# Two buffers for two output tiles and products for two taps in the last stage of a fused forward and backward kernel

## The chip, the cores and the metric

The kernel runs on one core of a Trainium2 chip. The metric is device time in microseconds (us), from runs on the chip, with the median of several. A profiled execution gives one trace, with times counted from the start of its span. The engines are TensorE (PE, with its weight loads as PEld), VectorE (DVE), ScalarE (ACT), GpSimd (POOL) and SyncE (SP), which mostly issues DMAs. Each engine runs its instructions in the order in which they were put into its queue.

## The reference

The forward pass adds a residual, a long convolution gated by a layer norm (an H3 block, A) and a bilinear gated feed-forward block (B). The kernel returns its output and the gradients of nine inputs for a given `grad_out`. The shapes are S = 2048 rows, D = 512 columns, F = 1376 hidden columns, 4 shift taps, all in bf16.

```python
xn = layernorm(A_q)
# A: q = xn
k_shift[s] = sum over t of k[s - 3 + t] * shift_k[:, 3 - t]
kv = k_shift * v
y = irfft(rfft(kv, 2S) * rfft(ssm_k, 2S))[:S] + kv * ssm_D
# B
h = (xn @ w_gate) * (xn @ w_up)
out = A_q + xn * y + h @ w_down
# returned: out, and its gradients by A_q, A_k, A_v, A_shift_k, A_ssm_k, A_ssm_D, w_gate, w_up, w_down
```

For the part that is changed, these lines matter. With `dks` the gradient by `k_shift`, the gradient by k is a sum of four products, row s being `sum over j of dks[s + j] * shift_k[:, j]`. The gradient by `shift_k` is, for each tap, the sum over the rows of `dks` times the shifted k. The gradient by A_q is a layer-norm backward pass over `grad_out * y` plus the feed-forward's part, plus `grad_out` itself.

## The kernel before

Rows are laid out as 128 partitions with R = 16 rows each, so a pass b from 0 to 7 works on the two rows 2b and 2b + 1 of every partition, and an operation on both rows has 128x1024 elements.

The work has three stages. The first (to about 110 us) normalises, makes the tables of the discrete Fourier transform and does the first halves of the transforms. The second (to about 300 us) runs the feed-forward block chunk by chunk (`ffn1`, `yb`) with the spectral products in between (`g_fwd`, `g_mul`, `g_inv`); its products land in DRAM (`HDD`, `BX`, `GD`). The third stage, which holds all of the change, starts with the line `wy_es.close()` and runs from about 316 us. There the main generator `dw()` takes the eleven hidden blocks fb in turn: `down_grad(fb)` (tile pd, gradient of w_down), transposes of the hidden values (`hid_t`, tile pt; for the last three blocks a transposing DMA, tile natT, and `last_t`), and the gradients of w_gate and w_up (tile pu). At each `yield` of `dw()` four side generators are moved on by a table of start and step:

```python
sides = [every(seq(inv_y(), load_dk()), 0, 3), every(dsk_gram(), 27, 2), every(inv_dk(), 35, 3), every(ew(), 10, 3)]
```

- `inv_y()` finishes the inverse transforms: `st1p` makes the tiles yC and dd through PSUM tile pq, and VectorE multiplies dd with v into `dks` (L948) and with the shifted k into kb (L949), which is stored to out_3. The last two calls use rows 12 to 15.
- `dsk_gram()` makes the gradient by `shift_k`: for each of four column groups TensorE fills the PSUM tile pk from `dks` and k (khC), VectorE takes its diagonal into the tile kd (L1077) and sums it (L1079); at the end dskb is transposed (pts) and copied into dskt.
- `inv_dk()` makes the gradient by ssm_k (tiles po, o5t) and, in `put_dD`, the gradient by ssm_D (ptd, dDt).
- `ew()` runs the list `tail`: final(0), final(1), bwd(0), final(2), bwd(1), and so on to final(7), bwd(6), bwd(7). `final(b)` makes two rows of the output (tile o) and of the gradient by A_q (tile e, with a float32 tile dxn), from yC, xnC, goC and a tile bb that `load_fin` loads from BX one pass ahead. `bwd(b)` makes two rows of the gradient by k (tile dk, with the tile tk for a product).

The stores of o, e and dk are not issued by the pass itself: they go into the list `late` and are issued by `put_late()` at the beginning of the next pass, on SP's queue. Nearly every other DMA of this stage is on that queue too. The DMAs use eight completion semaphores in rotation, so a DMA waits for the landing of the one that used its semaphore before.

The order of instructions on each engine isn't the order of the program text: the tile framework schedules them by priority, with its own estimate of times, and blocks under `tc.high_priority(offset=SOON)` are drawn forward. Buffers come from pools: c2 has one buffer for each name (`bufs=1`), c2b two; a new tile under a name (or a `tag`) waits until all readers of the tile that had the buffer before are done, a store's DMA among them. The last half of the last `down_grad` is copied by VectorE and stored by SP:

```python
for h, cp, q in ((0, act, nc.scalar), (1, dve, nc.sync)):
    hc = slice(256 * h, 256 * h + 256)
    cp(od[:fw, hc], pd[:fw, hc])
    q.dma_start(out_9[f0:f0 + fw, hc], od[:fw, hc])
```

Of the kernel before, what the change touches and what calls it, by code (L numbers as in the profile page):

```python
# [8 lines left out]
BF = mybir.dt.bfloat16  # L9
F32 = mybir.dt.float32  # L10
I32 = mybir.dt.int32
ALU = mybir.AluOpType
# [6 lines left out]
D = 512  # L19
F = 1376  # L20
R = 16
P = 128
NC4 = 4
# [167 lines left out]
def kernel(  # L191
# [24 lines left out]
    nc = tc.nc  # L216
# [20 lines left out]
    def dve(o, i):  # L237
        nc.vector.tensor_copy(o, i)  # L238
# [13 lines left out]
    def P2(name, shape, dt=F32):  # L252
        return ps2.tile(shape, dt, name=name, tag="p2")

    def P1(name, shape, dt=F32):
        return ps1.tile(shape, dt, name=name, tag="p1")
# [5 lines left out]
    skb = const.tile([P, 4, D], BF, name="skb")  # L262
# [640 lines left out]
    c2b = ctx.enter_context(tc.tile_pool(name="c2b", bufs=2, side="right", reuse_waits="tile"))  # L903
    c2 = ctx.enter_context(tc.tile_pool(name="c2", bufs=1, side="right", reuse_waits="tile"))
    yC = c2.tile([P, R, D], BF, name="yC")
    dks = c2.tile([P, R + 3, D], BF, name="dks")
# [158 lines left out]
    def dsk_gram():  # L1065
        for c in range(NC4):
            pk = P2("pk", [P, 2, D])
            for r in range(R):
                for h in range(2):
                    c0 = c * 128 + 64 * h  # L1070
                    nc.tensor.matmul(pk[64 * h:64 * h + 64, h, 0:256], lhsT=dks[:, r, c0:c0 + 64],
                                     rhs=KH[0][:, r:r + 4, c0:c0 + 64], start=(r == 0), stop=(r == R - 1))
            kd = c2.tile([P, 4, 64], F32, name="kd")
            with tc.high_priority(offset=SOON):
                for h in range(2):
                    hs = slice(64 * h, 64 * h + 64)
                    nc.vector.tensor_tensor(kd[hs], pk[hs, h, 0:256].rearrange("q (j c) -> q j c", j=4),  # L1077
                                            ident[hs, hs].unsqueeze(1).to_broadcast((64, 4, 64)), op=ALU.mult)
                nc.vector.tensor_reduce(dsk[:, c, :], kd[:], axis=AX.X, op=ALU.add)  # L1079
            yield  # L1080
        dskb = c2.tile([P, 4, NC4], BF, name="dskb")
        nc.vector.tensor_copy(dskb[:], dsk[:].rearrange("q c i -> q i c"))
        for _ in range(2):
            yield
        pt = P1("pts", [P, 4, P], BF)
        for j in range(4):
            nc.tensor.transpose(pt[:NC4, j, :], dskb[:, 3 - j, :], ident[:])
        dskt = c2.tile([NC4, P, 4], BF, name="dskt")
        dve(dskt[:], pt[:NC4].rearrange("c j q -> c q j"))
        nc.sync.dma_start(out_4.rearrange("(c p) j -> c p j", p=128), dskt[:])  # L1090
        yield

    def bwd(b):
        rb = slice(2 * b, 2 * b + 2)
        dk = c2b.tile([P, 2, D], BF, name="dk")
        t = c2.tile([P, 2, D], BF, name="tk", tag="dxn")
        for j in range(4):
            src = dks[:, 2 * b + j:2 * b + j + 2, :]
            w = skb[:, j:j + 1, :].to_broadcast((P, 2, D))
            if j == 0:  # L1100
                nc.vector.tensor_tensor(dk[:], src, w, op=ALU.mult)
            else:
                nc.vector.tensor_tensor(t[:], src, w, op=ALU.mult)  # L1103
                nc.vector.tensor_tensor(dk[:], dk[:], t[:], op=ALU.add)  # L1104
        late.append((o2_n[:, rb, :], dk))

    FL = {}
# [2 lines left out]
    def load_fin(b):  # L1110
        bb = c2b.tile([P, 2, 2, D], BF, name="bb")
        nc.sync.dma_start(bb[:], BX[:, 2 * b:2 * b + 2, :, :])
        FL[b] = bb

    def final(b):
        if b + 1 < 8:
            load_fin(b + 1)
        bb = FL.pop(b)
        rb = slice(2 * b, 2 * b + 2)
        tt = nc.vector.tensor_tensor  # L1120
        stt = nc.vector.scalar_tensor_tensor
        o = c2.tile([P, 2, D], BF, name="o0")
        tt(o[:], xnC[:, rb], yC[:, rb], op=ALU.mult)
        tt(o[:], o[:], bb[:, :, 0, :], op=ALU.add)
        late.append((o0_n[:, rb, :], o))
        e = c2.tile([P, 2, D], BF, name="e")
        tt(e[:], goC[:, rb], yC[:, rb], op=ALU.mult)
        dxn = c2.tile([P, 2, D], F32, name="dxn")
        for i in range(2):
            r = 2 * b + i  # L1130
            stt(dxn[:, i], e[:, i], 1.0, bb[:, i, 1, :], op0=ALU.mult, op1=ALU.add, accum_out=s1[:, r:r + 1])
            stt(e[:, i], dxn[:, i], 1.0, xnC[:, r, :], op0=ALU.mult, op1=ALU.mult, accum_out=s2[:, r:r + 1])
        nc.vector.tensor_scalar(m2[:, rb], s2[:, rb], -1.0 / D, None, op0=ALU.mult)
        stt(m1[:, rb], s1[:, rb], -1.0 / D, rstd[:, rb], op0=ALU.mult, op1=ALU.mult)
        for i in range(2):
            r = 2 * b + i
            stt(dxn[:, i], xnC[:, r, :], m2[:, r:r + 1], dxn[:, i], op0=ALU.mult, op1=ALU.add)
            nc.vector.tensor_scalar(e[:, i], dxn[:, i], rstd[:, r:r + 1], m1[:, r:r + 1], op0=ALU.mult, op1=ALU.add)
        tt(e[:], e[:], goC[:, rb], op=ALU.add)
        late.append((o1_n[:, rb, :], e))  # L1140
# [16 lines left out]
    for b in range(8):  # L1157
        tail.append(lambda b=b: final(b))
        if b > 0:
            tail.append(lambda b=b: bwd(b - 1))  # L1160
    tail.append(lambda: bwd(7))

    def put_late():
# [16 lines left out]
    def load_dk():  # L1180
        gks.append(load_gk(0))
        gks.append(load_gk(1))
        yield

    sides = [every(seq(inv_y(), load_dk()), 0, 3), every(dsk_gram(), 27, 2), every(inv_dk(), 35, 3), every(ew(), 10, 3)]
    for n, _ in enumerate(dw()):
        for sd in sides:
# [36 lines left out]
```

## Time and profile before

| what | us |
|---|---|
| median of 3 runs (lowest to highest) | 491.06 (489.58 to 493.37) |
| the profiled execution, its own time | 491.36 |
| its span | 489.6 |
| TensorE, weight loads busy | 470.8, 313.9 |
| VectorE, ScalarE, GpSimd busy | 341.1, 317.2, 15.4 |
| stage from 330 to 480: VectorE busy | 106.4 of 150 |
| bytes moved by DMA | 139.87 MB, 286 GB/s |

An engine's busy time is the sum of its instructions' time in the trace; matmuls are pipelined, so TensorE's is not a measure of its peak. The granted clock of TensorE is 0.99 on the mean. An engine's wait names what released it. A line such as L235 or L238 is that of the helper `act` or `dve`, through which all plain copies go, so copies are told apart by their tiles. "To landing" of a DMA counts from its issue to the moment at which its semaphore is set.

### The profile page before, as it was taken

Reading aid. Unit: us, or ns where it says so; the run is one execution under the profiler, and the core shown is the slowest. Engines: PE = TensorE matmul, PEld = TensorE weight load, DVE = VectorE, ACT = ScalarE, POOL = GpSimd, SP = SyncE. Lnnn points to the kernel's source line nnn. Section 1 sums busy time; section 2 is a strip of 40 time slices with the busy share of each in tenths; the row PEclk is TensorE's granted clock in tenths of the full one; section 3 lists DMA queues with packets and bytes.
Section 4 is the critical chain, followed back from the end, with each engine's and each line's share of the span. In section 5 each row is a group of like instructions: output and inputs, shape, how many; then the busy total and the mean of one; then the engine's idle time right before and its main releaser. Section 6 shows DMA issues by size and latency. Waiting matters only on the chain.

```text
span 489.6 us, 10516 instructions
## 1 busy us (share of the span) xinstructions
PE 470.8 (96%) x4335; PEld 313.9 (64%) x4335; DVE 341.1 (70%) x623; ACT 317.2 (65%) x353; POOL 15.4 (3%) x31
## 2 busy tenths in 40 slices
PE   7998999999999999999999999999999999999992
PEld 7866754547647457357357734577677778777790
DVE  6889979987275667677687873021270999998895
ACT  4876896769568678789689953567557522733320
POOL 8010000000000000000000000020000000000000
PEclk9999999999999999999999999999999999999996
DMA  8999999999997979788977199989999898999518
GB/s 272 376 380 347 304 257 330 330 317 327 313 300 229 255 233 242 242 260 251 287 240 239 62 368 321 352 313 350 325 367 362 301 326 270 311 310 229 191 55 283
DMA packets 105773, 139.87 MB, mean 286 GB/s; under 512 B 33371, under 2 KB 78848, under 8 KB 104062
## 3 DMA queue, kind: packets, MB, share of 16 engines
q1 hardware_dynamic: 104142, 137.84, 86.2%
q10 hardware_dynamic: 1584, 1.36, 0.9%
q8 instruction: 34, 0.56, 0.5%
q14 instruction: 13, 0.11, 0.1%
HBM read 68.45 MB, written 63.41 MB: 269 GB/s over the span
## 4 chain that ended last, share of the span: by engine, by line
PE 56%; DVE 21%; DMA 17%; issue 2%; ACT 2%; SPq 1%; DVEq 0%; ACTq 0%
PE px L553 14%; PE pgu L510 12%; PE py L546 7%; PE pdh L516 6%; PE pu L1048 3%; DMA out_dram<-o 3%; PE pf L368 3%; PE ps L582 3%; PE pg L611 3%; PE pd L1012 2%; DMA go_b<-in_grad_out_dram 2%; DVE tk L1103 2%; DMA HDD<-hd 2%; DVE dk L1104 2%; DMA hb<-HDD 2%
## 5 line engine op out<-in xcount | busy, mean ns | idle before, releaser
L553 PE MATMUL px<-WT,hd 128*128 128x512 bf16 (+1 forms) x352 | 81.1, 380 | 0.0
L1048 PEld LDWEIGHTS <-xnC 128*128 128x128 bf16 x704 | 67.1, 98 | 8.8 <-issue 0.9
L553 PEld LDWEIGHTS <-hd 128*128 128x128 bf16 (+1 forms) x352 | 32.8, 98 | 44.4 <-issue 7.7
L1048 PE MATMUL pu<-natd,xnC 128*128 128x256 bf16 x512 | 58.5, 273 | 0.2 <-ACT nath L235 0.2
L235 ACT CAST GO<-pg 128x1024 bf16<-128x1024 f32 x48 | 46.2, 1015 | 13.8 <-issue 7.2
L235 ACT CAST SP<-ps 128x1024 bf16<-128x1024 f32 x47 | 45.6, 1025 | 13.8 <-PE ps L582 11.9
L235 ACT CAST gu<-pgu 128x1024 bf16<-128x1024 f32 (+1 forms) x48 | 45.4, 945 | 13.8 <-PE pgu L510 13.4
L510 PE MATMUL pgu<-xt,Wu 128*128 128x256 bf16 (+1 forms) x352 | 53.1, 273 | 0.6 <-DVE fst L238 0.4
L598 DVE TENSOR_TENSOR T<-SP 128x2048 bf16<-128x2048 bf16 x24 | 29.4, 1223 | 34.8 <-ACT SP L235 34.7
L510 PE MATMUL pgu<-xt,Wg 128*128 128x256 bf16 (+1 forms) x352 | 52.8, 273 | 0.5 <-DMA Wg<-in_B_w_gate_dram 0.5
L516 PE MATMUL pdh<-gt,WdT 128*128 128x256 bf16 (+1 forms) x352 | 47.1, 273 | 0.1
L510 PEld LDWEIGHTS <-Wu 128*128 128x128 bf16 (+1 forms) x352 | 33.0, 100 | 14.5 <-issue 9.8
L546 PE MATMUL py<-Wd,hd 128*128 128x512 bf16 (+1 forms) x176 | 41.4, 380 | 0.0
L235 ACT CAST fst<-pf 128x1024 bf16<-128x1024 f32 x40 | 39.0, 1031 | 0.8 <-ACT dh L235 0.5
L235 ACT COPY natd<-pt 128x2048 bf16<-128x2048 bf16 x16 | 30.0, 1874 | 14.2 <-PE pt L845 14.2
L235 ACT CAST og<-pu 128x1024 bf16<-128x1024 f32 (+1 forms) x11 | 10.9, 993 | 43.4 <-PE pu L1048 36.6
L516 PEld LDWEIGHTS <-WdT 128*128 128x128 bf16 (+1 forms) x352 | 34.9, 100 | 5.2
L510 PEld LDWEIGHTS <-Wg 128*128 128x128 bf16 (+1 forms) x352 | 34.8, 100 | 4.4 <-DMA Wg<-in_B_w_gate_dram 0.8
L531 DVE TENSOR_TENSOR hd<-gu,dh 128x1024 bf16<-128x1024 bf16 (+1 forms) x48 | 30.8, 643 | 0.8
L530 DVE TENSOR_TENSOR hd<-gu 128x512 bf16<-128x512 bf16 (+1 forms) x48 | 19.1, 398 | 17.7 <-ACT gu L235 17.7
L1012 PE MATMUL pd<-goC,nath 128*128 128x512 bf16 x128 | 30.1, 379 | 0.0
L546 PEld LDWEIGHTS <-hd 128*128 128x128 bf16 (+1 forms) x176 | 16.4, 98 | 20.5 <-issue 3.1
(176 smaller groups left out, 702.4 us busy)
## 6 DMA issues: line engine op xcount, KB each, us to landing
HDD<-hd SPq DMA_DIRECT2D x35, 384.0 KB, 4.2
FD<-fst SPq DMA_DIRECT2D x24, 512.0 KB, 4.4
X<-FD SPq DMA_DIRECT2D x24, 512.0 KB, 5.0
GD<-GO SPq DMA_DIRECT2D x24, 512.0 KB, 4.1
g<-GD SPq DMA_DIRECT2D x11, 1024.0 KB, 8.5
hb<-HDD SPq DMA_DIRECT2D x8, 1344.0 KB, 8.5
bb<-BX SPq DMA_DIRECT2D x8, 512.0 KB, 6.6
BX<-bx SPq DMA_DIRECT2D x7, 512.0 KB, 4.1
```

The costliest lines, as they stand in the source:

```text
L235: nc.scalar.copy(o, i)
L368: nc.tensor.matmul(pf[:, c, :], lhsT=TB.W1[:, c, :], rhs=src[:, i, :], start=True, stop=not point)
L510: nc.tensor.matmul(pgu[:w, i, t, :], lhsT=W[:, c, f0:f0 + w], rhs=xt[:, :, c, :], start=(c == 0), stop=(c == NC4 - 1))
L516: nc.tensor.matmul(pdh[:w, i, :], lhsT=WdT[:, c, f0:f0 + w], rhs=gt[:, :, c, :], start=(c == 0), stop=(c == NC4 - 1))
L530: nc.vector.tensor_tensor(hd[:fw, fb0:fb0 + n, 0, :], gu[:fw, :n, 0, :], gu[:fw, :n, 1, :], op=ALU.mult)
L531: nc.vector.tensor_tensor(hd[:fw, fb0:fb0 + n, 1:3, :], gu[:fw, :n], dh[:fw, :n].unsqueeze(2).to_broadcast((fw, n, 2, 256)), op=ALU.mult)
L546: nc.tensor.matmul(py[:], lhsT=hd[:fw, fb, 0, ss], rhs=Wd[:fw, fb, :], start=(fb == 0), stop=(fb == NFB - 1))
L553: nc.tensor.matmul(px[:], lhsT=hd[:fw, fb, t, ss], rhs=W[:fw, fb, :], start=(t == 1 and fb == 0), stop=(t == 2 and fb == NFB - 1))
L582: nc.tensor.matmul(ps[32 * q:32 * q + 32, a, :], lhsT=TB.EF[64 * a:64 * a + 64, 4 * g + q, ri].rearrange("p k j -> p (k j)"), rhs=X[64 * a ...
L598: tt(W[:].rearrange("p c a d -> p c (a d)"), A[:, i:i + 1].rearrange("p c a d -> p c (a d)").to_broadcast((P, 2, 2 * D)), B[:].rearrange(" ...
L1012: nc.tensor.matmul(pd[:fw, :], lhsT=nat_h(fb, r), rhs=goC[:, r, :], start=(r == 0), stop=(r == R - 1))
L1048: nc.tensor.matmul(pu[:, c, :, :fw], lhsT=xnC[:, r, cs(c)], rhs=nat_d(fb, r), start=(r == 0), stop=(r == R - 1))
```

## The change

Three edits, all in the last stage.

1. `final(b)`: the tiles o and e get two buffers each (`bufs=2`) in place of one.
2. `dsk_gram()`: the tiles kd and dskt leave the pool c2, where each had one buffer of its own, and take the two buffers of the tile dd in c2b (`tag="dd"`). The last og1 uses the same tag, before and after.
3. `bwd(b)`: in place of a product for each of the four taps and three additions, there is one product for two taps at a time. Its source is an access pattern on dks in which the row step stands twice: element (u, i) is row 2b + j + u + i, so that the rows of the two taps overlap. The weights are two rows of skb, each repeated over the two output rows. The tile tk grows from 2 to 4 rows; it shares its buffer with the float32 tile dxn, which has that size.

```diff
-            kd = c2.tile([P, 4, 64], F32, name="kd")
+            kd = c2b.tile([P, 4, 64], F32, name="kd", tag="dd")
...
-        dskt = c2.tile([NC4, P, 4], BF, name="dskt")
+        dskt = c2b.tile([NC4, P, 4], BF, name="dskt", tag="dd")
...
     def bwd(b):
         rb = slice(2 * b, 2 * b + 2)
         dk = c2b.tile([P, 2, D], BF, name="dk")
-        t = c2.tile([P, 2, D], BF, name="tk", tag="dxn")
-        for j in range(4):
-            src = dks[:, 2 * b + j:2 * b + j + 2, :]
-            w = skb[:, j:j + 1, :].to_broadcast((P, 2, D))
-            if j == 0:
-                nc.vector.tensor_tensor(dk[:], src, w, op=ALU.mult)
-            else:
-                nc.vector.tensor_tensor(t[:], src, w, op=ALU.mult)
-                nc.vector.tensor_tensor(dk[:], dk[:], t[:], op=ALU.add)
+        t = c2.tile([P, 2, 2, D], BF, name="tk", tag="dxn")
+        for j in (0, 2):
+            s = dks[:, 2 * b + j:2 * b + j + 3, :]
+            (part, row, elem) = s.ap
+            src = bass.AP(s.tensor, s.offset, [part, [row[0], 2], [row[0], 2], elem])
+            w = skb[:, j:j + 2, :].unsqueeze(2).to_broadcast((P, 2, 2, D))
+            nc.vector.tensor_tensor(t[:], src, w, op=ALU.mult)
+            nc.vector.tensor_tensor(dk[:], t[:, 0] if j == 0 else dk[:], t[:, 1 if j == 0 else 0], op=ALU.add)
+            if j:
+                nc.vector.tensor_tensor(dk[:], dk[:], t[:, 1], op=ALU.add)
         late.append((o2_n[:, rb, :], dk))
...
-        o = c2.tile([P, 2, D], BF, name="o0")
+        o = c2.tile([P, 2, D], BF, name="o0", bufs=2)
...
-        e = c2.tile([P, 2, D], BF, name="e")
+        e = c2.tile([P, 2, D], BF, name="e", bufs=2)
```

Nothing outside these lines differs; after bwd's head the line numbers of the changed kernel are one higher. In the text below, o(b), e(b), bb(b) and dk(b) are the tiles of pass b, and kd(0) to kd(3) those of the four column groups.

## The prediction

> **What bounds the kernel now.** I read the page first, then the timeline of the last 28 us, the table by stage, the waits of VectorE (DVE) and TensorE (PE), and single groups. The page:
>
> ```profile
> PE 470.8 (96%) x4335; PEld 313.9 (64%) x4335; DVE 341.1 (70%) x623; ACT 317.2 (65%) x353; POOL 15.4 (3%) x31
> L598 DVE TENSOR_TENSOR T<-SP 128x2048 bf16<-128x2048 bf16 x24 | 29.4, 1223 | 34.8 <-ACT SP L235 34.7
> ```
>
> TensorE is busy 96% of the span, and a row of 32 matmuls of 256 columns (pu) takes 3.49 us wherever it stands in the chain, so it works at an even pace: what can be won lies in its few waits and behind its last matmul. The end, from the timeline (start, length, engine, line):
>
> ```profile
> 479.26 0.59 PE L1012 MATMUL pd<-goC,nat 128*96 128x512 bf16 x2
> 479.93 0.37 ACT L235 CAST od<-pd 96x256 bf16<-96x256 f32 x1 [2.70 <-PE pd L1012]
> 481.53 0.36 ACTq L1025 DMA_DIRECT2D out_dram<-od  x1
> ...
> 482.96 0.69 DVE L1104 TENSOR_TENSOR dk<-dk,tk 128x1024 bf16<-128x1024 bf16 x1
> 483.57 0.41 DVE L238 CAST od<-pd 96x256 bf16<-96x256 f32 x1
> 483.68 0.33 SPq L1165 DMA_DIRECT2D out_dram<-dk  x1
> 484.10 1.67 SPq L1059 DMA_DIRECT2D out_dram<-og  x2
> 485.87 0.56 SPq L1025 DMA_DIRECT2D out_dram<-od  x1
> ```
>
> TensorE ends at 479.85. ScalarE copies its half of the last od at once; the other half waits on VectorE, which is still in bwd(7) and gets to it at 483.57. SyncE (SP), whose queue is in order, has the last dk store ahead of og and od, so od leaves at 485.87 and the span closes at 489.6, 3.7 us later. VectorE ends the kernel. Why it is late:
>
> ```profile
> 390.00:410.00 20.00, 19.67 (x230) 15.77 (x229) 19.00 (x39) 7.54 (x6) 0.00 (x0) 1.00 0.89 300
> 430.00:450.00 20.00, 19.76 (x182) 14.74 (x181) 18.79 (x39) 7.54 (x8) 0.00 (x0) 1.00 1.05 262
> DVE o L1123 <- DMA out_dram<-o: 15.3, 2, 14.8
> DVE dks L948 <- ACT dd L235: 12.9, 1, 12.9
> DVE o L1124 <- DMA bb<-BX: 8.3, 1, 8.3
> DVE e L1127 <- DMA out_dram<-e: 4.2, 3, 3.1
> ```
>
> The first two rows are stages: length and PE busy, PE loads, DVE, ACT, POOL, clock, DMA share. VectorE is 95% busy from 390 to 450 because it idled before: 14.8 us of final(1), 365.0 to 379.8, for the store of final(0)'s o to free the one buffer. The e buffer costs 4.2 more later. Two waits of TensorE on VectorE belong to the same lateness:
>
> ```profile
> PE pt L845 <- DVE kd L1077: 0.3, 1, 0.3
> PE ptd L1003 <- DVE dskt L238: 0.2, 1, 0.2
> ```
>
> **The change part by part.** The instruction orders of TensorE, ScalarE and GpSimd stay as they are; VectorE's and SP's move, both only in the last stage (after 320 us).
>
> *Products for two taps.* A bwd was 7 operations of 128x1024, now it is 2 of 128x2048 and 3 of 128x1024: 16 instructions fewer. In the timeline an operation of 1024 starts 0.60 us after one that it does not depend on and 0.72 after one that it does; an old bwd is 0.60 + 6 x 0.72 = 4.9 us. The new product isn't in this trace. Below, the T row: same size, one broadcast operand, 1.23, with starts 1.14 apart. Above, one element per lane and cycle, as the float32 row L1131 has it (512 in 0.61): 4 x 0.6 = 2.4 us. I take 1.2, since the nearest row
>
> ```profile
> L531 DVE TENSOR_TENSOR hd<-gu,dh x48: 411/686/694, 13.8 to 280.9; 128x1024 bf16<-128x1024 bf16 x40, 96x512 bf16<-96x512 bf16 x8
> ```
>
> has a step of zero between rows in one operand, as the weights here, and keeps 0.69 for 1024. So 1.2 + 0.72 + 1.2 + 0.72 + 0.72, about 4.5: 0.4 less per bwd, 3 us in all, or 15 more at 2.4. (The Trainium skill, Vector Engine (DVE) Microarchitecture Reference, "Performance modes", gives two results a cycle to 16-bit operands of unit step and saw it with a row read again, which L531 agrees with; it lists "input rows that overlap", which the source dks has here, among what was not measured. That is my last rival.)
>
> *Two buffers for o and e.* No operation is added. The products o(1) and e(1) now come at about 323 us, in idle time. I go through VectorE's new order with the spacings above. Final(1) starts at 365.0 (its bb, issued at 357.86, lands a median 6.6 later) and ends 0.6 + 5.75 later, 371.3; bwd(0) to 375.8. Now o(2) waits for the store of o(0), since SP's queue up to that store is unchanged: 379.8. The wait is moved and cut from 14.8 to 4.0, not gone. Then three operations, 1.8, and the rest of final(2), 5.1: 386.7. The last dks need vb, issued from 378.2 and landing 7.1 later, 386.5: no wait. Five operations to 389.8 (before, they ended at 391.3, with final(2) and most of bwd(0) still to do). bwd(1) with o(3) and e(3) between, 5.5: 395.3; kd(0) 0.85. The rest of final(3) needs bb(3), issued behind the last kb store at 390.2, so 396.8 by the median. 5.5 later comes kd(1), 402.3 to 403.2; TensorE wants its bank at 403.87, and before got it at 404.15. kd(3) ends at 417.4 (wanted 418.2), dskt at 434.2 (wanted 435.9). TensorE gets back 0.3 + 0.1 + 0.2; I count 0.55.
>
> After that VectorE waits only for bb(7). It sits in SP's queue behind the two transposing loads natT; issued by 452.3 as before, it lands by 458.9, and final(7) 6.4 with two bwd of 4.5 ends by 474.3, some 5 us ahead of TensorE. That cover carries the costs I set to nothing: the 4.0 wait, bb(7), and up to 5 us of bad luck.
>
> *The small tiles in dd's buffers.* kd and dskt follow dd by then: dd's readers are on VectorE itself, before kd in order, and og1 comes long after dskt. With two buffers nothing new is waited for: 0. Were it to bind, it would be a kd, priced below.
>
> *SP's queue.* Stores move: o, e and dk of a pass stand further ahead, e(6) and dk(5) now before an og store, dk(0) between two kb stores. What is queued behind is hb (issued 392.8 and 410.4, used some 10 us later), bb, the loads of the last gk, and natT. Each store's data is ready, by the walk above, before SP reaches it, while before SP sat 22.3 us on e and 14.2 on dk. The 512 KB o5t stores, which left at 476.6 and 480.9, leave at about 466 and 472.5; between 460 and 480 the DMA engines are 20 to 40% busy, so there is room.
>
> *The new end.* TensorE ends at 479.85 - 0.55 = 479.3. ScalarE's half 0.08 + 0.37: 479.75, its store at once (before it waited until 481.5 for a dk store that uses the same DMA semaphore in the program; now the earlier user is an o5t store), 3.4 to landing and 1.3 to close: 484.4. VectorE's half waits for ScalarE's half: 479.8 to 480.2; SP issues at 480.3, and 3.7 later is 484.0. I take 484.2: 489.6 - 484.2 = 5.4 us less. Bounds: nothing from TensorE and a slow last store, 4.5; all of TensorE's waits and a store landing in 2.4 from ScalarE, 6.4. (The Trainium skill, DMA: Bandwidth & Descriptors, "Anatomy of one DMA", fits another issuing path with 2.0 us plus bytes over 436 GB/s, by estimate 2.1 for 48 KB, where this trace has 2.4 and 3.4; by it the end would be 0.3 to 1.3 us sooner.) The profiled execution took 491.36 around its span of 489.6; 491.36 - 5.4 = 485.96. It stood 0.30 above the median of 491.06, so the forecast is 485.7.
>
> **Rivals.** *A load decides kd(1).* bb has landed between 3.7 and 10.2 after its issue. At 10.2, bb(3) comes at 400.4, kd(1) ends at 406.8, and TensorE waits 2.9 at pt; kd(3) and dskt then follow without a further wait. 485.7 + 2.9 = 488.6. For it: the DMA share is 0.89 and more from 330 to 450. Against: the median, and 0.7 us to spare.
>
> *It doesn't do what it says.* The o(0) store is slow under the khC load (it landed 11.7 after issue) and would gate VectorE again with two buffers, and bb(7) at the end: VectorE then stays last. Only if it loses all of the 5 us does the end move back; with 3 us lost beyond that, 488.7; with nothing gained 491. Against: by 390 final(2) is done too, over 6 us of work.
>
> *The product for two taps runs at one element a cycle* (the other side). Place: seven products stand before dskt, and TensorE's transpose ptd waits for it. With x us extra per product dskt ends at 434.2 + 7x against 435.9, TensorE is late by 7x - 1.7, and the end comes at 484.2 + that. At x = 1.2 it is 6.7 late, span 490.9, time 492.4 on the median; with dependent spacing (x = 1.7), 495.9. It is slower than before from x = 1.0, that is from a product of 2.2 us. For it: overlapping source rows, which no row shows. Against: L531 and the T row.
>
> **How the numbers follow.** The forecast has 0.66, with its own range 484.3 to 487.3; the load 0.12, no relief 0.06, the slow product 0.13, slower by something not named 0.03. One per cent of 491.06, about what a measurement of this kernel can tell from no change, is 4.9: below 486.15 is faster. Of the forecast's 0.66 about 0.10 lies above that: faster 0.56. Within 1%: 0.10 + 0.12 + 0.06 + 0.07 of the slow product (near 492) = 0.35; slower: its other 0.06, where a late load comes on top, + 0.03 = 0.09. The range from 484.0 to 492.4 leaves out 0.07 of the slow product and the unnamed, and some 0.08 of the forecast's low end.
>
> **What would show it.** Right: the last dk of VectorE ends between 469 and 475, od on VectorE starts within 1 us of the last matmul, SP's od store issues near 480.3, no o wait over 5 us, product rows of 1.2 us. Wrong in a step: a product above 2 us; kd or dskt in TensorE's waits with more than 1 us; the last matmul after 481; VectorE still busy at 479; a last store landing 4 us or more after issue.

## The result, and the profile after

The changed kernel takes 483.74 us (median of 6 runs, 482.98 to 484.74) where the kernel before took 491.1 beside it (6 runs, 488.39 to 494.22): a ratio of 0.985, with a 95% interval of 0.981 to 0.989. The forecast was 485.7 with a lower end of 484.0. The direction, and TensorE as the new bound, came as forecast; the gain is about 2 us larger, and 483.74 lies below that lower end. The profiled execution took 484.36, with a span of 482.6, against 491.36 and 489.6 before: 7.0 us less, where the sum had 5.4.

The page after, first the busy times, then the chain that ended last:

```profile
PE 471.6 (98%) x4335; PEld 314.6 (65%) x4335; DVE 339.6 (70%) x607; ACT 317.1 (66%) x353; POOL 15.3 (3%) x31
...
PE 71%; DVE 14%; DMA 10%; SPq 2%; issue 1%; ACT 1%; DVEq 0%; ACTq 0%
```

VectorE has 16 instructions and 1.5 us less. The share that matters is TensorE's in the chain of waits: 71% of the span, where it was 56% (and VectorE 21%) in the kernel before:

```profile
PE 56%; DVE 21%; DMA 17%; issue 2%; ACT 2%; SPq 1%; DVEq 0%; ACTq 0%
```

The end of the timeline:

```profile
478.54 0.59 PE L1012 MATMUL pd<-goC,nat 128*96 128x512 bf16 x2
479.21 0.37 ACT L235 CAST od<-pd 96x256 bf16<-96x256 f32 x1 [2.70 <-PE pd L1012]
479.61 0.36 ACTq L1025 DMA_DIRECT2D out_dram<-od  x1
479.62 0.42 DVE L238 CAST od<-pd 96x256 bf16<-96x256 f32 x1 [9.96 <-ACT od L235]
480.06 0.34 SPq L1025 DMA_DIRECT2D out_dram<-od  x1
```

Before, VectorE got to its half of the last od 3.7 us after the last matmul, out of a full queue. Now it has been idle for 9.96 us when ScalarE releases it, and TensorE ends the kernel. VectorE's waits after 300 us (total, count, longest):

```profile
DVE dks L948 <- ACT dd L235: 18.6, 2, 14.1
DVE o L1125 <- DMA bb<-BX: 15.2, 4, 7.8
DVE o L1124 <- ACT yC L235: 12.1, 1, 12.1
DVE od L238 <- ACT od L235: 10.0, 1, 10.0
DVE bx L548 <- PE py L546: 9.4, 2, 6.4
DVE o L1124 <- DMA out_dram<-o: 1.9, 1, 1.9
```

The wait for o's store is 1.9 us instead of 15.3, and e's store is not in the list any more. The idle time didn't vanish: it now stands at the end (10.0), and in waits for bb, which has become the limit of a final because VectorE comes to it sooner. And the new product:

```profile
L1102 DVE TENSOR_TENSOR tk<-dks,skb 128x2048 bf16<-128x2048 bf16 x16 | 19.5, 1220 | 0.3
```

### The profile page after: what moved, and what is told of

It reads as the page before. It is cut to its first block, busy times and chain, and to the rows that moved or that the text cites. A ratio compares the mean times of both kernels' runs of the same rounds, so it can differ in the third digit from the quotient of the medians.

```text
span 482.6 us, 10498 instructions
## 1 busy us (share of the span) xinstructions
PE 471.6 (98%) x4335; PEld 314.6 (65%) x4335; DVE 339.6 (70%) x607; ACT 317.1 (66%) x353; POOL 15.3 (3%) x31
## 4 chain that ended last, share of the span: by engine, by line
PE 71%; DVE 14%; DMA 10%; SPq 2%; issue 1%; ACT 1%; DVEq 0%; ACTq 0%
PE px L553 14%; PE pgu L510 13%; PE pu L1048 11%; PE py L546 7%; PE pdh L516 6%; PE pd L1012 6%; DMA bb<-BX 3%; PE ps L582 3%; PE pg L611 3%; PE pt L845 2%; PE pf L368 2%; DMA HDD<-hd 2%; DMA vb<-in_A_v_dram 2%; DVE fst L238 2%; PE pq L918 1%; PE po L987 1%
## 5 line engine op out<-in xcount | busy, mean ns | idle before, releaser
L235 ACT CAST SP<-ps 128x1024 bf16<-128x1024 f32 x47 | 45.6, 1026 | 13.8 <-PE ps L582 11.9
```

The costliest lines, as they stand in the source:

```text
L235: nc.scalar.copy(o, i)
```

## The experiments

The theory after the result (A): one wait for a store's buffer made VectorE late; with it gone TensorE ends the kernel, and VectorE has 10 us to spare. Open were which of the three edits does it, whether the spare time is real, and why the gain was larger than the sum. Each ratio in the table is to runs of the kernel before taken beside that kernel; their medians are 491.1 to 492.5.

| kernel | median, us (lowest to highest) | ratio to before (95%) |
|---|---|---|
| the whole change, first runs | 483.74 (482.98 to 484.74) | 0.985 (0.981 to 0.989) |
| e1: both buffers and the move, products as before | 484.12 (483.81 to 484.31) | 0.983 (0.980 to 0.986) |
| e2: the products alone | 489.81 (488.19 to 492.15) | 0.995 (0.993 to 0.997) |
| e4: all but e's second buffer | 489.79 (488.98 to 491.86) | 0.995 (0.993 to 0.998) |
| e4: all but o's second buffer | 484.25 (482.75 to 484.95) | 0.983 (0.979 to 0.986) |
| e5: seven products more | 485.29 (484.61 to 487.25) | 0.989 (0.985 to 0.993) |
| e5: fourteen products more | 493.24 (491.02 to 494.53) | 1.004 (1.002 to 1.006) |
| e7: five stores ahead of the last | 485.46 (485.03 to 485.75) | 0.988 (0.984 to 0.992) |
| e8, e10: e's second buffer alone, twice | 486.55 (484.34 to 487.43), 486.04 (485.47 to 486.18) | 0.990 (0.987 to 0.993), 0.987 (0.981 to 0.992) |
| e9: the whole change, beside e10 | 483.82 (483.13 to 485.27) | 0.983 (0.978 to 0.988) |
| e11: e alone, hb on ScalarE's queue | 521.02 (520.64 to 523.25) | 1.059 (1.053 to 1.065) |
| e12: the change, hb so, od in halves | 520.22 (519.29 to 522.57) | 1.057 (1.051 to 1.063) |
| e13: e and the move | 485.08 (484.49 to 486.19) | 0.989 (0.984 to 0.994) |
| e14: e and the products | 485.59 (484.59 to 486.61) | 0.989 (0.983 to 0.995) |
| e15: the move alone | 492.12 (490.28 to 493.20) | 1.001 (0.998 to 1.004) |
| e16: the change, od in halves | 483.99 (482.87 to 488.33) | 0.988 (0.981 to 0.995) |

**Buffers or products?** e1 is the change with bwd as it was; e2 is the kernel before with the new bwd alone.

> The two buffers for o and e, with kd and dskt in dd's buffers (which makes room for them), bwd as before the change. Theory A (the wait for the store of o(0) and e(0) made VectorE last; with two buffers it ends some 10 us ahead of TensorE, so its own work no longer counts): the old bwd costs VectorE 0.4 us each, which the idle time ahead of the last od covers; VectorE ends near 470.5, TensorE sets the end, time 484 to 485, as with the whole change (483.74). Rival B (the 16 instructions saved are part of what moved the end): the 3 us that they take come back at the end, time near 487.

> Only the products for two taps; o and e have one buffer each, kd and dskt their own. Theory A: VectorE still idles about 14.8 us for the store of final(0) and is last; the 0.4 us saved on each of eight bwd come off its end, which was 483.98, so od leaves some 3 us earlier: time near 488, VectorE's last dk near 481. Rival B, in its strong form (VectorE's work sets the end and the wait is filled): near 485. Rival C (what bwd saves is lost again in waits for stores): 491, as before.

The buffers give the gain. The last dk of e1 is ready near 470.4, and 9.2 us of idle time stand ahead of its last od:

```profile
479.56 0.42 DVE L238 CAST od<-pd 96x256 bf16<-96x256 f32 x1 [9.15 <-ACT od L235]
```

The products alone take 2.2 us off the time (489.81 against 491.97 beside it), less than theory A had. VectorE's wait for o's store is still there in e2:

```profile
381.22 0.69 DVE L1124 TENSOR_TENSOR o<-xnC,yC 128x1024 bf16<-128x1024 bf16 x1 [15.45 <-DMA out_dram<-o]
```

From the end of this wait to its last od VectorE needs 101.8 us (381.22 to 483.06), 2.0 less than before the change (379.78 to 483.57). But in these two profiles the wait ends 1.4 us later in e2, so that od starts only 0.5 earlier.

**Which buffer?** Each is the changed kernel with one word taken out again:

```diff
-        o = c2.tile([P, 2, D], BF, name="o0", bufs=2)
+        o = c2.tile([P, 2, D], BF, name="o0")
```

and, in the other, the same at e.

> The whole change, but e with one buffer; o has two. Theory A: the stores of o(0) and e(0) leave 0.4 us apart and land together, so the wait moves from o(1) to e(1) and stays near 14 us; VectorE is last again, time 487 to 489, near the kernel with the products for two taps alone. Rival D (the waits add up as the table of waits has them, 15.3 us for o and 4.2 for e, so that o's buffer brings most): 484 to 485, a wait of some 4 us at e.

> The whole change, but o with one buffer; e has two. Theory A: o(1) waits until the store of o(0) has landed, near 380, as before the change; time 487 to 489. Rival D (e's buffer takes away its 4.2 us, which came late, after 420, where nothing makes up for it, and so brings most of the gain): 484 to 485.

Here the theory was half wrong. Without o's second buffer nothing is lost; without e's all but 2.2 us is (489.79 against 491.97 beside it), and that much the products give alone. VectorE's timeline around final(1), first with e's buffer alone doubled:

```profile
367.15 0.69 DVE L1132 SCALAR_TENSOR_TENSOR dxn<-e,bb 128x512 f32<-128x512 bf16 x1 [3.07 <-DMA bb<-BX]
...
376.86 0.69 DVE L1105 TENSOR_TENSOR dk<-dk,tk 128x1024 bf16<-128x1024 bf16 x1
379.87 0.69 DVE L1124 TENSOR_TENSOR o<-xnC,yC 128x1024 bf16<-128x1024 bf16 x1 [2.32 <-DMA out_dram<-o]
```

and with o's alone doubled:

```profile
366.43 0.69 DVE L1125 TENSOR_TENSOR o<-o,bb 128x1024 bf16<-128x1024 bf16 x1 [3.08 <-DMA bb<-BX]
378.85 0.69 DVE L1124 TENSOR_TENSOR o<-xnC,yC 128x1024 bf16<-128x1024 bf16 x1 [11.72 <-DMA out_dram<-o]
379.46 0.69 DVE L1128 TENSOR_TENSOR e<-goC,yC 128x1024 bf16<-128x1024 bf16 x1
```

Nothing in a pass reads o except the addition of bb and its store. All of the pass's layer-norm work, and with it bwd in the order, hangs on e. With e doubled, final(1) runs on from 367 while o's product waits behind it and finds its buffer nearly free. With o doubled, only o's own two operations come early; e(1) still waits for e(0)'s store, which SyncE issues right behind o(0)'s, and the o(2) that the order puts ahead of it wears the wait's name. With o doubled, e(0)'s store was issued at 366.82 and landed 12.5 us later, at 379.3; e(1) starts at 379.46. e's one buffer by itself thus holds VectorE as long as the row shows, to 0.2 us: the row "o <- out_dram<-o 14.8" named the tile that stood first in the queue, not the one that mattered.

**Are VectorE's 10 us to spare?** The changed kernel with extra work ahead of the last od:

```diff
+        if b == 7:
+            for _ in range(7):
+                nc.vector.tensor_tensor(t[:], src, w, op=ALU.mult)
```

> The changed kernel with seven more products of 128x2048 (1.23 us each, 8.6 us in all, their results unused) at the end of the last bwd, ahead of VectorE's half of the last od. Theory A (TensorE ends the kernel, and VectorE waits 10.0 us for the last od): 483.7 to 484.8 us, the idle time before the last od down from 10.0 us to about 1.4, nothing else moved. Rival B (VectorE's last stretch still decides by some wait that the trace does not show): about 8 us more, 492.

> The changed kernel with fourteen such products (17.2 us). Theory A: the 10.0 us are used up and 7.2 us are left over, so the last od of VectorE starts near 486.9 instead of 479.6 and the time is 490.5 to 491.5 us, about that of the kernel before. Rival B: 500.

With seven, the idle time ahead of od falls from 9.96 to 1.16, and VectorE's half still starts when ScalarE's ends. The median is 0.5 us above theory A's range and far from rival B's 492. The kernel's profile has TensorE waiting 1.66 us for a load of hb, a thing of its own that is taken up below; 483.5 less 1.66 is a span of 481.8, no longer than the changed kernel's. With fourteen VectorE ends the kernel again:

```profile
478.22 0.59 PE L1012 MATMUL pd<-goC,nat 128*96 128x512 bf16 x2
...
486.00 0.41 DVE L238 CAST od<-pd 96x256 bf16<-96x256 f32 x1
486.44 0.34 SPq L1025 DMA_DIRECT2D out_dram<-od  x1
```

The profiled execution took 491.02, as expected; the median, 493.24, is 2 us more than that. The kernel before has such a spread too (488.4 to 495.5 in its runs beside all of these), while the runs of the changed kernel lie between 483.0 and 485.3. Where the spread of the kernels that VectorE ends comes from stays open.

**Why is the end shorter than the sum had it?** In the changed kernel the last store stands in an empty queue. Five stores like og's (96 KB each, into a scratch tensor) are put in front of it:

```diff
...
+            for z in range(5):
+                nc.sync.dma_start(SCR[z], LG["o1"][:, z % 2, :, :96])
```

> The changed kernel with five more stores of the kind of og (128 partitions x 4 rows of 192 bytes, 96 KB each, into a scratch tensor) in SyncE's queue right ahead of the last od's store; nothing else is changed. Theory A (the last store lands 1.5 us after its issue because nothing is queued ahead of it; before, it took 2.4 because og's stores stood ahead): the last od's store lands 2.4 us or more after its issue, and the span is 0.9 to 2 us longer: 484.7 to 485.8 us. Rival B (the shorter landing is no matter of what is queued): landing 1.5 us and 483.7 us as in the changed kernel.

The time is in the range of theory A, but by another way. The five issues hold SyncE from 477.48 to 480.84, so od's store is issued 0.88 later (480.94); it lands 1.8 us after its issue instead of 1.5, and the span is 1.2 longer. So stores ahead cost mostly the time in which SyncE issues them, and only 0.3 in landing, 0.24 of it in od's own issue (0.58 instead of 0.34). Of the 0.9 us by which the last store of the kernel before took longer to land, two thirds aren't explained by this. Busy DMA engines alone don't explain them either: their share is 0.99 from 485 to 487 in the kernel before and also 0.99 from 481 to 482 here, against 0.04 to 0.27 from 479 to 482 in the changed kernel. What differs is what they move, 379 and 220 GB/s in the two microseconds of the kernel before and 165 here. Large stores in flight (o5t's, of 512 KB each, are issued from 480.86 in the kernel before) are a rival that no run tests.

**Is e's buffer all of it?** One word changed in the kernel before:

> The kernel before with one word changed: e in two buffers, everything else as before (o one buffer, products of one tap, kd and dskt in their own tiles). Theory A (the wait that mattered was that of final(1)'s first step on e(0)'s store; with e in two buffers the layer norm's chain runs on and the product of o stands behind it; the shorter products and o's second buffer give nothing once TensorE ends the kernel): 484 to 485 us, the last dk ready near 470, the last od of VectorE 0.4 us behind ScalarE's, e's waits for its store gone and one wait of 2 to 3 us of o's product left. Rival B (the shorter products or the move of kd and dskt are needed as well): 486 to 488 us, with VectorE's half of the last od more than 2 us behind the last matmul.

> The kernel before with e in two buffers and nothing else, a second time. Theory A (e's second buffer is the whole gain; the 486.6 of the first time held TensorE's wait for hb, 1.4 us in its profile, which has nothing to do with the edit): runs from 484 where hb comes in time to 487 where it doesn't; a profile without the hb wait has its last matmul near 479.3 and a span of 482 to 483. Rival B (the other two edits bring 1 to 3 us of their own): a profile without the hb wait still has a span of 484 or more, and VectorE's last dk is later than 474.

> The changed kernel itself, as the measure for the three others on the same chip: 483 to 485 us, TensorE's last matmul ending near 479.1 and the load of hb that follows khC issued at 368.9 and not waited for, unless SyncE's issue of kb's two stores at 363 takes 3.1 us instead of 1.6 (as in three of the profiles so far); then TensorE waits 1.2 to 1.8 us for hb at 385.5 and the time is by that much longer.

It gives most of the gain (4.6 and 6.5 us against the kernel before beside it), but not all: 486.0 against 483.8 on the same chip, and 486.55 is above theory A's 484 to 485. VectorE is out of the way in both (9.1 and 9.4 us idle ahead of od). What differs is mainly one wait of TensorE, 1.42 us in e8's profile and 0.95 in e10's; here DVE, then SP, then PE of e8:

```profile
365.33 0.69 DVE L948 TENSOR_TENSOR dks<-dd,vb 128x1024 bf16<-128x1024 bf16 x1 [1.56 <-DMA vb<-in_A_v_dram]
...
371.28 0.41 SPq L791 DMA_DIRECT2D hb<-HDD  x1
...
387.26 0.96 PE L845 MATMUL pt<-ident,hb 128*128 128x128 bf16 x14 [1.42 <-DMA hb<-HDD]
```

and in the changed kernel:

```profile
363.01 0.69 DVE L948 TENSOR_TENSOR dks<-dd,vb 128x1024 bf16<-128x1024 bf16 x1
...
368.90 0.43 SPq L791 DMA_DIRECT2D hb<-HDD  x1
...
385.41 0.78 PEld L845 LDWEIGHTS <-hb 128*128 128x128 bf16 x14 [0.35 <-DMA hb<-HDD]
385.42 0.95 PE L845 MATMUL pt<-ident,hb 128*128 128x128 bf16 x14
```

A load of vb comes 1.6 us late, VectorE makes the second kb later, SyncE's second kb store waits for it, and khC's three loads and hb stand behind that store. TensorE gets hb 16.0 us after its issue here (371.28 to 387.26), behind khC's 2.4 MB. In the changed kernel it is issued 2.4 us earlier and comes just in time: the weight loads waited 0.35 us for it at 385.41, the matmuls not. From the same product of down_grad to its last matmul TensorE takes 145.95 us in e10's profile (334.00 to 479.95) and 144.03 in e9's (335.43 to 479.46); the waits for hb (0.95) and for kd (0.4) make up most of these 1.9 us. (The expectation of e9 put the longer stretch at 363 down to SyncE's issuing. Each of the two issues takes 0.34; what is longer is the second's wait for VectorE.) Is it one of the other two edits that keeps hb in time?

> The kernel before with e in two buffers and kd and dskt in dd's tiles; o one buffer, the products as before. Theory C (the move of kd and dskt shortens the loads of the stretch from 346 to 370, so that hb comes in time): 483.5 to 484.8 us, hb's second issue under 1.7 us, VectorE not waiting for vb at 363, TensorE not waiting for hb at 385. Theory D (the shorter products do it): 485.5 to 487 us, with the wait for hb.

> The kernel before with e in two buffers and the products of two taps; o one buffer, kd and dskt in tiles of their own. Theory C (the move is what helps): 485.5 to 487 us, with the waits for vb and hb as in e alone. Theory D (the products): 483.5 to 484.8 us without them.

> The kernel before with nothing but kd and dskt in dd's tiles; the order of the instructions is that of the kernel before on every engine. VectorE ends this kernel by its wait of 14 us for o's store, whatever TensorE does. Theory C: hb's second issue and the waits for vb as short as in the whole change, and by that at most 1 us off the time, 489.5 to 491.5. Theory D: nothing moves, 490.5 to 492.5.

The profile of e13 has no such wait and a span of 482.7; that of e14 has 1.81 us of it and a span of 484.6. But each kernel has runs on both sides (spans of 482.7 to 484.3 and of 482.6 to 484.6), e15 shows that the move alone is worth nothing, and two kernels with all three edits have the wait in their profiles: 1.66 in the one with seven products more, and 2.93 in e16 below. Neither C nor D is shown. What is shown: with the same three edits the wait comes and goes (neither profile of the changed kernel itself has it), and less the wait, the spans of e alone (483.5 and 483.4), e14 (482.8) and e16 (483.6) are within 1 us of the changed kernel's own 482.6 and 483.5. A late vb isn't its only way: in e14 and e16 VectorE waits only 0.4 and 0.2 us for vb, and TensorE gets hb 17.4 and 17.1 us after its issue. Why e alone had the wait in both its profiles stays open.

**Taking hb out of SyncE's queue.** One line decides the queue:

```diff
-        nc.sync.dma_start(t[:fw], HDD[:fw, fb])
+        (nc.scalar if fb > 2 else nc.sync).dma_start(t[:fw], HDD[:fw, fb])
```

> The same kernel (e alone in two buffers) with the loads of hb in the last stage issued by ScalarE's queue, behind its copy of og, instead of SyncE's queue behind the stores and khC's loads. Theory A (the surplus of e alone is TensorE's wait for hb, which stands in SyncE's queue behind slow issues): hb is issued near 367 instead of 369 to 371, no wait for hb, 483.5 to 485 us in all runs. Rival B (the wait is not set by the queue but by the transfer of khC's 2.4 MB): hb lands no sooner, the wait of 1 to 2 us stays in a part of the runs, 484 to 487.

> The changed kernel with hb's loads on ScalarE's queue as in the run before, and with the last down_grad as two products of 256 columns, each with its own tile in PSUM and in SBUF, so that ScalarE copies and stores the first half while TensorE still makes the second, and VectorE copies the second half without waiting for ScalarE's copy (0.41 us between the two starts in the changed kernel). Theory A (TensorE's end and the chain behind it set the time): the last store is issued 0.9 us after the last matmul's end instead of 0.93 + 0.41, the span is 0.3 to 0.6 us shorter than the changed kernel's on the same chip, 483.0 to 484.0 us. Rival B (the two halves cost TensorE more than that, 14 to 16 more weight loads in the last stretch): no gain or up to 1 us more.

Both theories missed by some 35 us in each run. ScalarE's timeline of e11:

```profile
369.70 1.01 ACT L235 CAST og<-pu 128x1024 bf16<-128x1024 f32 x1 [2.75 <-PE pu L1048]
378.19 0.37 ACTq L791 DMA_DIRECT2D hb<-HDD  x1
378.60 1.86 ACT L235 COPY natd<-pt 128x2048 bf16<-128x2048 bf16 x1 [7.88 <-DMA bb<-BX]
```

The issue of hb waits, and in ScalarE's queue the copy of natd, which TensorE needs next, stands behind it: 7.9 us here, 6.5 at the next one (the row books the wait to natd, though the issue ahead of it had it, and names a load of bb). SyncE's order changed as well, and TensorE waits for g three times (1.3 to 2.6 us) and, longest of all, for VectorE's kd (8.2 and 5.5 us); VectorE in turn waits 16.9 us for a load of bb and 11.4 for a store of e. So these two say nothing of their questions. They show that a DMA issue that waits holds the copies behind it; how much of the 35 us comes from that, and how much from the changed order, isn't separated.

**The chain behind the last matmul.** VectorE's half waits for ScalarE's copy of the other columns of the same PSUM tile. Two tiles of 256 columns end that:

```diff
+        for h, cp, q in ((0, act, nc.scalar), (1, dve, nc.sync)):
...
+            pd = P1("pd", [P, 256])
+            for r in range(R):
+                nc.tensor.matmul(pd[:fw, :], lhsT=nat_h(fb, r), rhs=goC[:, r, hc], start=(r == 0), stop=(r == R - 1))
...
```

> The changed kernel with the last down_grad as two products of 256 columns with a tile each in PSUM and in SBUF: ScalarE copies and stores the first half while TensorE makes the second, and VectorE's copy of the second half doesn't stand behind ScalarE's. Theory A: VectorE's copy starts 0.1 us after the last matmul's end instead of 0.5, and the span is 0.3 to 0.6 us shorter than the changed kernel's 481.1 to 483.5: 483.0 to 484.0 us. Rival B (twice the weight loads in the last product cost TensorE as much): 483.7 to 484.7 us.

The step does what it should, here ScalarE, TensorE and VectorE:

```profile
481.89 0.37 ACT L235 CAST od<-pd 96x256 bf16<-96x256 f32 x1 [0.99 <-PE pd L1034]
...
483.18 0.38 PE L1034 MATMUL pd<-goC,nat 128*96 128x256 bf16 x2
483.60 0.42 DVE L238 CAST od<-pd 96x256 bf16<-96x256 f32 x1 [10.81 <-PE pd L1034]
```

VectorE starts 0.04 us after the last matmul's end (0.49 in the changed kernel), and the 32 matmuls of half the width take 3.66 us where the 16 took 3.61. That is 0.4 us won at the end, too little to measure: three runs have 482.87 to 484.55, and the profiled one, which waited 2.93 for hb, has 488.33. No version here is measurably faster than the changed kernel.

## Where the prediction held, and the step that failed

The step that failed is the term for the new end: the time from the issue of the last store to the end of the span. I kept the 3.7 us of the kernel before; it measured 2.5 (480.06 to 482.6). These 1.2 us alone put the time below the range, since 483.74 + 1.2 is above its lower end of 484.0. Why the store landed sooner is in part open (below). The bound, and how the change moves it, came as forecast, but for which of the two buffers matters. The parts in turn:

*What bounds the kernel:* right. VectorE ended it, through a wait for a store's buffer. But I put 14.8 us down to o's buffer and called e's cost 4.2, "later". The experiments show that e's buffer holds the chain; o's wait stood in front of it. In the trace before, e(0)'s store landed at 380.4 (issued at 368.53, 11.9 to landing), 0.6 behind o(0)'s, so that e's buffer alone would have held final(1) as long. For the whole change this made no difference, since both were doubled.

*Products:* right. 1.22 us, as the T row's 1.223, where I took 1.2; the slow product is refuted, and a bwd with the first spacing went from 4.9 to 4.65 (373.74 to 378.39), so that 0.27 us are saved per bwd, 2 us in all, where I had 0.4 and 3. (At 2.4 us a product the sum would have given 16 us more, not 15.) The source with overlapping rows, which the Trainium skill's "Performance modes" (Vector Engine (DVE) Microarchitecture Reference) lists as not measured, runs at the pace of the other 16-bit rows here. On the end the products are worth nothing that could be measured (e1 against the whole change).

*VectorE's walk:* right to about 1 us up to dskt. Final(1) began at 367.38 and not at 365.0, for bb(1) came 10.4 us after its issue and not 6.6; the wait for o(0)'s store took that up and was 1.9 instead of 4.0. The last step came 4.6 us early, since bb(7) was issued at 448.79 and not at 452.3, and came 5.1 later instead of 6.6.

| step | forecast | measured |
|---|---|---|
| o(2) comes free | 379.8 | 380.28 |
| kd(1) ends | 403.2 | 403.69 |
| kd(3) ends | 417.4 | 418.3 |
| dskt ends | 434.2 | 435.4 |
| last dk ends | 474.3 | 469.7 |

*The move of kd and dskt at nothing:* right (e15, 492.12 against 491.87); TensorE waits 0.2 for kd and not at all for dskt. (The 435.9 at which I had TensorE want dskt is the start of VectorE's copy in the trace before; TensorE was free for it at 436.4.)

*TensorE's end:* 479.13 against 479.3, partly by luck. I counted 0.55 back from kd and dskt, and 0.37 came. Another 0.36 was there before the changed stage begins: at 309 TensorE of the kernel before waited 0.67 for an earlier hb, and that of the kernel after didn't.

*SP's queue:* I wrote that hb is used some 10 us after its issue and looked at the later two loads. The one behind khC, issued at 368.9, has nothing to spare, and two kernels with all three edits lost 1.7 and 2.9 us by it. It belonged among the rivals.

*The new end:* this term was mis-sized. For the last store I kept the kernel before's 3.7 from issue to the span's end. But that store had dk's and og's right ahead of it and o5t's 512 KB stores from 480.86, and the new order takes them away; that o5t's would leave at about 466 and 472.5 I had written down myself (it was 465.9 and 471.6). Which of them made the landing slow is open: e7 gives stores like og's 0.3 of the 0.9. The landing of the last od's two stores, before and then after:

```profile
DMA to landing us min/median/max: 2.4/2.9/3.4
```

```profile
DMA to landing us min/median/max: 1.5/1.6/1.6
```

Then 1.0 to the close instead of 1.3. Against the sum: 0.24 from the earlier issue (480.06 for 480.3), 0.9 from the landing, 0.3 from the close, and 0.2 that I had added between the two halves (484.2 for 484.0): 1.64, and 5.4 + 1.6 is the measured 7.0. The profiled execution stood 0.62 above the median instead of 0.30, which is the rest of the way from 485.7 to 483.74. I had a hint and gave it a sentence: by the Trainium skill (DMA: Bandwidth & Descriptors, "Anatomy of one DMA"), with its fit for another issuing path, the end would come 0.3 to 1.3 us sooner. The trace now has 1.5 to 1.6, even less than the 2.1 estimated from that fit for these 48 KB.

*The range:* its lower end took the same slow landing with it, at 2.4. It also counted ScalarE's half alone; VectorE's store, issued 0.5 us later, would by the same numbers have ended later. The rivals didn't come: bb(3) was in time for kd(1), and no VectorE work reached the end.

## What to carry to other kernels

A wait row names the tile at the head of the queue; ask which tile's buffer the chain behind it really needs, and double that one. When an edit removes the engine that ended the kernel, rebuild the whole end from the new order, the landing of the last store included, since the old one may have been slow because of what stood ahead of it. And once the bound has moved to a steady engine, list every load that it uses with its landing and its margin: the smallest margin may be the next spread of the runs.

## What the runs showed of the hardware

An operation of 128x2048 in bf16 whose source rows overlap, with weights of step zero, takes 1.22 us, no more than one with separate rows (1.223). A 48 KB store issued into an empty queue landed 1.5 to 1.6 us later, 1.8 behind five stores of 96 KB, 2.4 to 3.4 in the kernel before, whose DMA engines were 99% busy from 485 to 487. Those five stores of 96 KB kept SyncE busy for 3.36 us. A DMA issue in ScalarE's queue that had to wait held the copies behind it for 6.5 to 7.9 us. Two tiles with one buffer each, stored one behind the other, showed as one wait of 14.8 us under the name of the first; a second buffer for the first, with the products, won 2.2 us, no more than the products alone, and a second buffer for the second alone 4.6 and 6.5.
